# Gate sums inside the score products of the first four heads, and other edits to the opening of a fused attention and two-layer kernel

## The chip, the cores and the metric

The kernel runs on one core of one Trainium2 chip, and the metric is the device time of one launch in microseconds (us). The core has TensorE (PE in the rows; its weight loads are PEld), VectorE (DVE), ScalarE (ACT), GpSimd (POOL) and SyncE (SP), whose queue issues nearly all of the DMAs. Each engine takes its instructions in the order in which the program gives them.

## The reference, cut to what matters

```python
scores = scale * np.matmul(q, k.transpose(0, 1, 3, 2))      # q, k: [4, 8, 576, 64], scale = 1/8
cum = np.cumsum(np.log(np.clip(f, 0.0001, 1.0)), axis=-1)   # f: [4, 8, 576], the gates
decay = cum[:, :, :, None] - cum[:, :, None, :]
scores = np.where(causal, -1e9, scores + decay)
attn = softmax(scores)                                      # the row maximum is subtracted first
x = matmul(attn, v)                                         # heads side by side: [2304, 512]
x = leaky_relu(x @ w_in, 0.01) @ w_out                      # moe_: 512 x 2048, 2048 x 512
return silu(x @ w_in2) @ w_out2                             # moe2_: the same sizes
```

The gate term of a query (`cum` at its own row) is the same for all keys of that row, so it falls out of the softmax; only the term of the key changes the result.

## The kernel before, in words

The program is written out by a planner (`Plan`): generators for each part of the work yield steps with an engine, an estimated cost and a rank, and a simulated clock decides the order in which the steps of one engine are emitted (a lower rank first, then the earlier request). The hardware then runs each engine in that order and waits on semaphores. A changed cost, rank or wait can so change the order of everything behind it.

Attention goes by batch and half of the sequence: the first 256 tokens (blocks of 128 queries with 128 and 256 keys) and the last 320 tokens. The first eight heads (`load_first`, n < 8) are the first half of batch 0. They are loaded in pairs into tiles `qk` with 66 rows: 64 rows of q or k and two rows for the gates. `gates` loads f (`fs`), clamps it on VectorE (line 351), takes logarithms on ScalarE (line 353) and multiplies by a triangle of 8.0 (`tri`, made by GpSimd in lines 333 and 334) on TensorE (line 368). That gives `cps`, 8 times the cumulative sums: two chunks of 128 tokens for the first 256 columns, five chunks for the last 320, as each half sums from token 0. `first_rows` copies the sums of the first half to `cfr` (lines 419 and 420) and sends them by eight small DMAs (line 132) into rows 64 and 65 of the `qk` tiles. A score product (`product` in `score`, line 606) is then one fp32 matmul over 66 rows. VectorE masks it and takes the row minimum (line 594), ScalarE the exponential (line 624), VectorE or ScalarE scales it (lines 632 and 634), TensorE transposes it (line 683), and a pair of heads is multiplied with v (line 752) and split into two parts into `ring` (lines 288 and 296).

`plain_rows` and `split_rows` store the sums of all 32 heads for the later heads (`cum_p`, `cum_d`), with copies on ScalarE and the other steps on GpSimd. When they are through, `gates` gives its tiles back, and room for the second weight matrix opens (`wo`).

`first_weights` brings 32 weight tiles of 512 KB, 16 of w_in and 16 of w_out, once the gate rows are sent (`wait("rows")`). Each is rebuilt to fp32 by `to_f32` (ScalarE line 1351, VectorE lines 1352, 1353 and 1355). The 16 tiles of w_in and the first two of w_out are then split into a rounded part (ScalarE, line 288) and a remainder (`less`: GpSimd line 295 or VectorE line 296, whichever the planner takes to end first). The first layer (`hidden`, line 882, and `summed`, lines 954 and 960) takes steps as weights and tokens come, beside the attention of the next heads. The second layer follows from about 600 us.

Of the kernel before, what the change touches and what calls it, by code (L numbers as in the profile page):

```python
# [34 lines left out]
C_LEAD = 3  # L35
FAVOR = 0.3
# [192 lines left out]
def fused_kernel(ctx, tc, qt, kt, va, vb, ft, w1, wi2, wo2, out):  # L229
# [69 lines left out]

    def build_consts():  # L300
        def mask(t, pattern, cmp, fill, base, mult):
            return lambda: nc.gpsimd.affine_select(
                out=t, in_=t, pattern=[pattern], compare_op=cmp, fill=fill, base=base, channel_multiplier=mult
            )

        for r in range(2):
            yield op("pool", 0.3, lambda: nc.gpsimd.memset(cum_rows[0][r][:, 1 - r], 1.0))
        signal("ones")
        yield op("pool", 0.6, lambda: nc.gpsimd.memset(zmask, 0.0))
        yield op("pool", 0.75, mask(zmask, [-1, ZOFF + 256], ALU.is_ge, -8.0 * MASK, ZOFF, 1))  # L310
        signal("zmask")
        for st in stats:
            yield op("pool", 0.1, lambda: nc.gpsimd.memset(st[:, 6:9], 1.0))
        yield op("pool", 0.15, lambda: nc.gpsimd.memset(ident, 1.0))
        yield op("pool", 0.25, mask(ident, [-1, 128], ALU.is_equal, 0.0, 0, 1))
        signal("ident")


    cum_rows = {}

    def gates(cp):
# [4 lines left out]
        tri = cp.tile([128, 512 + S], F32, name="tri")  # L326
# [4 lines left out]

        def triangle():
            yield op("pool", 0.95, lambda: nc.gpsimd.memset(tri, 8.0), 0)
            yield op("pool", 1.05, lambda: nc.gpsimd.affine_select(
                out=tri, in_=tri, pattern=[[1, 512 + S]], compare_op=ALU.is_ge,
                fill=0.0, base=-512, channel_multiplier=-1,
            ), 0)
# [9 lines left out]
        def logs(n, sl):  # L347
            src = ft[0:nfull * 128, :].rearrange("(c p) h -> p c h", p=128) if n == 128 else ft[nfull * 128:S, :]
            dst = fs[0:n, sl, :] if n == 128 else fs[0:n, nfull, :]
            yield dma(100e3, lambda: nc.sync.dma_start(out=dst, in_=src), 0)  # L350
            yield dve(64, lambda: nc.vector.tensor_scalar(
                fs[0:n, sl, :], fs[0:n, sl, :], 0.0001, 1.0, op0=ALU.max, op1=ALU.min), 0)
            yield act(128, lambda: nc.scalar.activation(fs[0:n, sl, :], fs[0:n, sl, :], ACTF.Ln), 0)

        yield par(warm_up(), triangle(), logs(*parts[0]), logs(*parts[1]))
        p.start(seq(op("act", 1.4, lambda: nc.scalar.activation(warm, fs[0:1, 0, 0:1], ACTF.Exp), 0)))
        pss = []
        banks = []
        for i, (t0, tn) in enumerate(HALF):
            banks.append((yield take(("av", "sp")[i], (1, 3)[i])))  # L360
            ps = ps_at.tile([H * B, tn], F32, tag=("av", "sp")[i], name="cps", bufs=(1, 3)[i])
            todo = [c for c in range(nfull + 1) if 128 * c < t0 + tn]

            def sums():
                for c in todo:
                    n = 128 if c < nfull else rem
                    o = 512 - 128 * c + t0
                    nc.tensor.matmul(  # L368
                        ps, fs[0:n, c, :], tri[0:n, o:o + tn], start=(c == todo[0]), stop=(c == todo[-1])
                    )  # L370

            yield op("pe", 2 * pe_cost(tn, 4) * len(todo), sums, 0)
            pss.append(ps)
            if i == 0:
                cf = cum_rows[0]
                p.start(first_rows(ps, cf))
        signal("cum")

        def plain_rows():
            yield pool(S, lambda: nc.gpsimd.memset(cp3[:, 1, :], 1.0))  # L380
            for i, ((t0, tn), ps) in enumerate(zip(HALF, pss)):
                w = slice(t0, t0 + tn)
                yield act(tn, lambda: nc.scalar.copy(cp3[:, 0, w], ps))
                if i == 0:
                    yield wait(("cf", 0), ("cf", 1))
                give(("av", "sp")[i], banks[i])
                yield pool(tn / 2, lambda: nc.gpsimd.tensor_scalar(
                    cp3[:, 2, w], cp3[:, 0, w], -1.0, 1.0, op0=ALU.mult, op1=ALU.mult))
# [3 lines left out]
        def split_rows():  # L392
            c, hi, lo = cp3[:, 0], cr[:, 0], cr[:, 1]
            yield pool(S, lambda: nc.gpsimd.memset(f32(cr[:, 2:4, :]), 1.0))
# [8 lines left out]
        yield from split_rows()  # L403
        signal("gates")

    def first_rows(ps, cf):

        def rows(r, step):
# [6 lines left out]
            ) for i in range(H // 2)])  # L415
# [3 lines left out]
            rows(0, act(256, lambda: nc.scalar.copy(cf[0][:, 0], ps[0:H]), 0)),  # L419
            rows(1, dve(256, lambda: nc.vector.tensor_scalar(cf[1][:, 1], ps[0:H], -1.0, None, op0=ALU.mult), 0)),  # L420
# [32 lines left out]
    def load_first():  # L453
# [3 lines left out]
        def group(i):  # L457

            t = first[i] = slot(i, [66, 2, 2, tn], F32, "qk0")
            def move(r, src):  # L460
                yield dma(131e3, lambda: nc.sync.dma_start(
# [1188 lines left out]
```

## Time and profile before

| | us |
|---|---|
| median of 3 runs | 1010.4 (1008.49 to 1010.43) |
| the profiled execution's own time | 1006.94 |
| its span, first to last instruction | 1005.2 |
| TensorE busy in it | 989.9 |
| VectorE, ScalarE, GpSimd busy | 772.9, 637.3, 141.1 |

Times in rows are us from the span's start unless marked ns. An fp32 matmul shows as two MATMUL records. "Busy" of TensorE is modelled from instruction ends, and it says nothing of the clock; the granted clock (PEclk) stands beside it, with 1.00 for 2.4 GHz and 0.50 for 1.2 GHz. In a timeline, the name behind "<-" in brackets is what ended the idle time before the piece.

### The profile page before, as it was taken

The numbers are of one execution on the slowest core, as the hardware profiler recorded it, in microseconds if no ns is written. First come the engines' busy times: TensorE is split into PE (matmuls) and PEld (weight loads), VectorE is DVE, ScalarE is ACT, GpSimd is POOL, SyncE is SP. The second block draws the span as 40 slices with busy tenths as digits, with TensorE's granted clock in tenths as the row PEclk, the third lists the DMA queues.
The fourth block names the chain that finished last, engine by engine and source line by source line (L and its number), as shares of the span: only waits on it lengthen the run. The fifth ranks groups of instructions, "written<-read, shape, count | busy, mean of one in ns | idle before, by whom it ended". The sixth has DMA issues, their size and how long they took to land.

```text
span 1005.2 us, 20884 instructions
## 1 busy us (share of the span) xinstructions
PE 989.9 (98%) x7786; PEld 943.5 (94%) x7786; DVE 772.9 (77%) x1818; ACT 637.3 (63%) x1385; POOL 141.1 (14%) x161
## 2 busy tenths in 40 slices
PE   8999999999999999999999999999999999999998
PEld 5667779999999999999999999999999999999997
DVE  4899867787788878878776989685832389998884
ACT  5666667767887678877774657565644576444441
POOL 2232002211222211342110212000000000000000
PEclk8799999999999999999999999999999999999999
DMA  5943423231242222332221876688873486445441
GB/s 166 339 125 108 170 69 109 75 97 41 62 131 77 68 72 58 100 97 70 85 70 69 272 269 235 216 293 315 293 254 134 158 292 181 147 142 153 126 127 63
DMA packets 98213, 148.98 MB, mean 148 GB/s; under 512 B 8296, under 2 KB 69376, under 8 KB 96032
## 3 DMA queue, kind: packets, MB, share of 16 engines
q1 hardware_dynamic: 98112, 147.65, 45.8%
q8 instruction: 61, 1.00, 0.4%
q14 instruction: 40, 0.33, 0.1%
HBM read 99.21 MB, written 43.66 MB: 142 GB/s over the span
## 4 chain that ended last, share of the span: by engine, by line
PE 89%; DVE 6%; issue 2%; ACT 1%; POOL 0%; DMA 0%; DVEq 0%; ACTq 0%; POOLq 0%
PE hps L882 19%; PE m L1317 18%; PE m L1161 18%; PE acc L960 17%; PE sps L606 6%; PE tps L683 5%; PE av L793 4%; PE acc L954 2%; PE av L752 1%; DVE ct L1353 1%; DVE sc L594 1%; DVE ct L1355 1%; PE cps L368 1%; DVE ct L1352 1%; DVE sc L632 1%
## 5 line engine op out<-in xcount | busy, mean ns | idle before, releaser
L882 PE MATMUL hps<-ring,w 128*128 128x256 f32 x1728 | 261.1, 288 | 0.0
L882 PEld LDWEIGHTS hps<-ring,w 128*128 128x128 f32 x1728 | 229.5, 192 | 5.5 <-issue 3.5
L960 PE MATMUL acc<-g,dec 128*128 128x256 f32 x1344 | 199.2, 285 | 1.4 <-DVE dec L296 1.4
L1161 PE MATMUL m<-xc,w 128*128 128x256 f32 x1536 | 185.4, 282 | 1.4 <-ACT u L1193 0.7
L1161 PEld LDWEIGHTS m<-xc,w 128*128 128x128 f32 x1536 | 184.2, 191 | 1.8 <-ACT u L1193 0.9
L1317 PE MATMUL m<-w,gc 128*128 128x256 f32 x1512 | 181.6, 283 | 0.0
L1317 PEld LDWEIGHTS m<-w,gc 128*128 128x128 f32 x1512 | 181.3, 191 | 0.2 <-DVE gc L296 0.2
L960 PEld LDWEIGHTS acc<-g,dec 128*128 128x128 f32 x1344 | 177.4, 191 | 2.0 <-DVE dec L296 1.6
L288 ACT CAST gc<-g 128x512 fp32r<-128x512 f32 (+1 forms) x144 | 80.0, 566 | 82.5 <-DVE g L1008 32.6
L624 ACT ACTIVATE sc<-sc,st 128x576 f32<-128x576 f32 (+4 forms) x160 | 93.1, 582 | 56.3 <-DVE st L594 54.8
L288 ACT CAST dec<-wo 128x512 fp32r<-128x512 f32 x112 | 69.4, 620 | 44.2 <-PE acc L960 42.8
L296 DVE TENSOR_TENSOR gc<-g,gc 128x512 fp32r<-128x512 f32 (+1 forms) x144 | 87.5, 619 | 12.4 <-ACT gc L288 11.1
L594 DVE CUSTOM_DVE_ANT_0 sc<-sps,zmask 128x288 f32<-128x288 f32 (+4 forms) x160 | 71.9, 450 | 30.2 <-PE sps L606 28.6
L683 PE MATMUL tps<-ident,sc 66*107 66x66 f32 (+3 forms) x480 | 70.4, 275 | 4.6 <-DVE st L643 2.1
L296 DVE TENSOR_TENSOR dec<-wo,dec 128x512 fp32r<-128x512 f32 x82 | 57.1, 697 | 20.7 <-ACT dec L288 20.3
L683 PEld LDWEIGHTS tps<-ident,sc 66*107 66x107 f32 (+3 forms) x480 | 56.4, 155 | 11.7 <-issue 3.5
L1008 DVE TENSOR_TENSOR g<-g 128x256 f32<-128x256 f32 x144 | 59.1, 419 | 7.2 <-DMA g<-g_d 6.3
L701 DVE TENSOR_TENSOR pl<-tps,pt 107x320 fp32r<-107x320 f32 (+2 forms) x114 | 54.2, 507 | 12.4 <-ACT pt L700 11.6
L295 POOL TENSOR_TENSOR dec<-wo,dec 128x512 fp32r<-128x512 f32 x30 | 42.7, 1423 | 145.1 <-ACT dec L288 120.0
L606 PE MATMUL sps<-m,s 68*128 68x288 f32 (+9 forms) x264 | 60.0, 308 | 0.1
L700 ACT CAST pt<-tps 107x320 fp32r<-107x320 f32 (+2 forms) x114 | 45.9, 446 | 16.8 <-PE tps L683 16.5
L296 DVE TENSOR_TENSOR g<-hps,g 128x512 fp32r<-128x512 f32 x65 | 44.6, 686 | 13.7 <-ACT g L288 13.1
(132 smaller groups left out, 1397.2 us busy)
## 6 DMA issues: line engine op xcount, KB each, us to landing
g_d<-z SPq DMA_DIRECT2D x16, 1024.0 KB
g<-g_d SPq DMA_DIRECT2D x32, 512.0 KB
w_d<-f SPq DMA_DIRECT2D x16, 896.0 KB
ws<-w_d SPq DMA_DIRECT2D x56, 256.0 KB
wst<-in_wi_dram SPq DMA_DIRECT2D x16, 512.0 KB
wst<-in_wo_dram SPq DMA_DIRECT2D x16, 512.0 KB
qk<-in_kt_dram SPq DMA_DIRECT2D x24, 288.0 KB
wss<-in_w_dram SPq DMA_DIRECT2D x10, 512.0 KB
```

Source lines behind the costliest of these rows:

```text
L288: ("act", act_cost(n, base), lambda: nc.scalar.copy(dst, src), 0.0),
L296: ("dve", dve_cost(n), lambda: nc.vector.tensor_tensor(dst, a, b, op=ALU.subtract), 0.0),
L594: yield dve(w, lambda: nc.vector.tensor_tensor_reduce(out=sc[0:qn, k0:k0 + w], in0=ps[0:qn], in1=zmask[0:qn, z0:z0 + w], scale=-0.125, sca ...
L606: nc.tensor.matmul(ps[0:qn], ht[x][:, qs], ht[y][:, k0:k0 + w], start=r == 0, stop=r == len(ops) - 1)
L624: yield act(kn, lambda: nc.scalar.activation(sc[0:qn, 0:kn], sc[0:qn, 0:kn], ACTF.Exp, scale=-1.0, bias=st[0:qn, 2 * i + a:2 * i + a + 1], ...
L683: nc.tensor.transpose(ps[0:k1 - k0, o:o + qn], ht["p"][i][0:qn, k0:k1], ident[0:qn, 0:qn])
L701: yield op("dve", dve_cost(width), lambda: nc.vector.tensor_tensor(pts[1][0:kw], ps[0:kw], f32(pt[0:kw]), op=ALU.subtract), 0, PE_LAT)
L882: nc.tensor.matmul(hp_t[:, part], w[:, wi, c * 128:(c + 1) * 128], x[xi][:, c, :], start=(part == 0 and c == 0 and r == 0), stop=(c == KC ...
L960: nc.tensor.matmul(o, w[:, wi, c * 128:(c + 1) * 128], g[:, gi, part * T:(part + 1) * T], start=(start and r == 0 and c % 2 == 0), stop=(s ...
L1008: ("dve", dve_cost(n), lambda: nc.vector.tensor_tensor(dst, a, b, op=op_), 0.0),
L1161: nc.tensor.matmul(dst[:, a], w[:, wi, c * 128:(c + 1) * 128], x[:, xi, c], start=start and a == 0 and c == 0 and r == 0, stop=stop and c ...
L1317: nc.tensor.matmul(banks[b][:, e], t[:, gi, a * 128:(a + 1) * 128], w[:, wi], start=begin and a == 0 and r == 0, stop=jp == NP // 2 - 1 an ...
```

## The change

For the first four heads (`DIRECT = 4`) a score product no longer reads gate rows. It takes the 64 rows of q and k, and then adds into the same PSUM bank, for each chunk of 128 keys, a matmul whose stationary operand is the logarithm column of that head spread over all queries, and whose moving operand is the triangle, now -8. The `qk` rows are sent for heads 4 to 7 only. The sums `cps` take only the chunks that begin in their own half; the last value of the first half is added afterwards on VectorE. GpSimd clamps f, and VectorE fills tiles that GpSimd filled before; GpSimd no longer takes remainders of weight tiles (`less(..., "d")`) nor the work on the rows for later heads, which VectorE and ScalarE do. One load of f and one of k are issued by ScalarE. Two tiles of w_in (`EARLY = 2`) are sent once heads 2 and 3 and the first v are sent, the others still after "rows". The end of `gates` also waits for the scores of the fourth head.

```diff
+DIRECT = 4
+EARLY = 2
 def build_consts():
+            yield from clamp(0)      # GpSimd: tensor_scalar max, min on fs
+            yield from clamp(1)
 def gates(cp):
-        tri = cp.tile([128, 512 + S], F32, name="tri")
+        tri = cp.tile([128, HALF[1][1]], F32, name="tri")
-            todo = [c for c in range(nfull + 1) if 128 * c < t0 + tn]
+            todo = [c for c in range(nfull + 1) if t0 <= 128 * c < t0 + tn]
-            yield op("pe", 2 * pe_cost(tn, 4) * len(todo), sums, 0)
+                yield op("pe", pe_cost(tn - lo, 4), sums, 0 if i == 0 else 1)
+                    yield dve(tn, lambda: nc.vector.tensor_scalar(
+                        cp3[:, 2, w], ps, cp3[:, 2, t0 - 1:t0], None, op0=ALU.add), 0)
-            yield pool(S, lambda: nc.gpsimd.tensor_tensor(lo, c, f32(hi), op=ALU.subtract))
+            yield dve(S, lambda: nc.vector.tensor_tensor(lo, c, f32(hi), op=ALU.subtract))
-                yield pool(S / 2, lambda: nc.gpsimd.tensor_scalar(dst, f32(src), -1.0, 1.0, op0=ALU.mult, op1=ALU.mult))
+                yield act(S, lambda: nc.scalar.mul(dst, f32(src), -1.0))
+        yield wait(("scored", DIRECT - 1, 1))
 def first_rows(ps, cf):
-            ) for i in range(H // 2)])
+            ) for i in range(DIRECT // 2, H // 2)])
 def load_first():
+                if i == 0 and r:
+                    yield op("act", 0.6, lambda: nc.scalar.dma_start(out=dst, in_=src_), 0, 2.0)
-            yield wait(("row", 0, i), ("row", 1, i))
+            if 2 * i >= DIRECT:
+                yield wait(("row", 0, i), ("row", 1, i))
 def product(ps, k0, w):
+            if n < DIRECT:
+                nc.tensor.matmul(ps[0:qn], ht["s1"][0:64, qs], ht["m1"][0:64, k0:k0 + w], start=True, stop=False)
+                for c in range(w // 128):
+                    nc.tensor.matmul(
+                        ps[0:qn, 128 * c:w], opened["fs"][:, c, n:n + 1].broadcast_to([128, qn]),
+                        opened["tri"][:, 0:w - 128 * c], start=False, stop=c == w // 128 - 1,
+                    )
+                return
 def conv_in(f):            # and in conv_out for f < RES
-        yield less(DM, w[:, 1], t, f32(w[:, 0]))
+        yield less(DM, w[:, 1], t, f32(w[:, 0]), "d")
 def first_weights():
-        yield wait("rows")
-
         def fetches(which):
+            if which:
+                yield wait("rows")
             for f in range(FF):
+                if f == EARLY:
+                    yield wait("rows")
                 yield from fetch(f, which)
+        yield wait(("prep", DIRECT - 1), "v0_sent")
```

## Rows read from the trace of the kernel before

**Rows 1.** The page, first part: busy us, share of the span, instructions.

```profile
PE 989.9 (98%) x7786; PEld 943.5 (94%) x7786; DVE 772.9 (77%) x1818; ACT 637.3 (63%) x1385; POOL 141.1 (14%) x161
```

**Rows 2.** Stretches: length; PE, PEld, DVE, ACT, POOL busy (count); clock, DMA share, GB/s.

```profile
10.70:16.50 5.80, 4.49 (x23) 2.90 (x22) 3.91 (x21) 4.47 (x17) 1.92 (x3) 0.97 0.36 98
16.50:26.20 9.70, 9.70 (x41) 6.77 (x41) 6.48 (x31) 7.07 (x24) 0.32 (x1) 0.50 0.88 293
26.20:29.90 3.70, 1.80 (x14) 1.08 (x13) 3.34 (x13) 3.32 (x11) 3.30 (x3) 0.96 1.02 363
29.90:43.20 13.30, 13.08 (x38) 7.67 (x39) 9.86 (x30) 7.34 (x19) 1.27 (x1) 0.50 1.01 341
43.20:60.00 16.80, 16.68 (x108) 12.84 (x107) 16.72 (x37) 12.80 (x26) 5.95 (x3) 0.99 0.48 155
60.00:100.00 40.00, 39.09 (x222) 28.14 (x222) 39.13 (x87) 26.05 (x58) 11.12 (x8) 1.00 0.47 137
200.00:300.00 100.00, 100.00 (x833) 99.77 (x832) 81.45 (x234) 76.31 (x197) 21.77 (x33) 1.00 0.30 85
```

**Rows 3.** Timeline of TensorE, 4 to 45 us: start, us, what, count.

```profile
4.63 6.12 PE L368 MATMUL cps<-tri,fs 128*32 128x256 f32 x14 [0.87 <-ACT fs L353]
10.68 2.15 PE L606 MATMUL sps<-qk 66*128 66x128 f32 x8
...
14.50 0.83 PE L606 MATMUL sps<-qk 66*128 66x128 f32 x4
15.17 0.49 PE L683 MATMUL tps<-ident,sc 128*128 128x128 f32 x3
...
24.48 1.49 PE L606 MATMUL sps<-qk 66*128 66x128 f32 x4
25.76 0.78 PE L683 MATMUL tps<-ident,sc 128*128 128x128 f32 x3
...
27.13 0.87 PE L752 MATMUL av<-pf,v 128*64 128x256 f32 x8
30.12 0.87 PE L683 MATMUL tps<-ident,sc 128*128 128x128 f32 x3 [2.12 <-DVE st L643]
...
40.58 2.93 PE L882 MATMUL hps<-ring,w 128*128 128x256 f32 x12
```

**Rows 4.** Timeline of SP and VectorE in the opening: clamps, gate rows, mask, weights.

```profile
2.78 1.38 DVE L351 TENSOR_SCALAR fs<-fs 128x128 f32<-128x128 f32 x2 [1.57 <-DMA fs<-in_ft_dram]
...
7.00 5.10 SPq L132 DMA_DIRECT2D qk<-cfr  x8
...
11.33 0.29 DVE L594 CUSTOM_DVE_ANT_0 sc<-sps,zmask 128x128 f32<-128x128 f32 x1 [3.97 <-PE sps L606]
...
18.58 1.96 SPq L1393 DMA_DIRECT2D wsr<-in_w_dram  x4
```

**Rows 5.** Groups of GpSimd over the span, by form: the splits of weights.

```profile
L295 POOL TENSOR_TENSOR w<-ct,w 128x512 fp32r<-128x512 f32 x11 | 17.9, 1629 | 51.8 <-ACT w L288 51.8
L295 POOL TENSOR_TENSOR wr<-ct,wr 128x512 fp32r<-128x512 f32 x1 | 1.8, 1802 | 2.6 <-ACT wr L288 2.6
```

**Rows 6.** Groups of VectorE, 20 to 130 us, by form: conversion and split.

```profile
L1353 DVE SCALAR_TENSOR_TENSOR ct<-cy,ct 128x512 int32<-128x512 int32 x16 | 12.9, 809 | 0.0
L1353 DVE SCALAR_TENSOR_TENSOR ct<-wo,ct 128x512 int32<-128x512 int32 x14 | 11.7, 837 | 0.2
L1355 DVE SCALAR_TENSOR_TENSOR ct<-wss,ct 128x512 int32<-128x512 int32 x10 | 9.0, 904 | 0.1
L296 DVE TENSOR_TENSOR w<-ct,w 128x512 fp32r<-128x512 f32 x5 | 3.4, 687 | 1.5 <-ACT w L288 1.5
```

**Rows 7.** Timeline: one GpSimd split, and VectorE instructions during and after it.

```profile
61.46 1.39 POOL L295 TENSOR_TENSOR w<-ct,w 128x512 fp32r<-128x512 f32 x1 [1.33 <-ACT w L288]
61.65 1.75 DVE L1353 SCALAR_TENSOR_TENSOR ct<-wo,ct 128x512 int32<-128x512 int32 x1
63.76 0.68 DVE L1353 SCALAR_TENSOR_TENSOR ct<-cy,ct 128x512 int32<-128x512 int32 x1
```

More of the change, by code (lines that the diff above doesn't have):

```diff
@@ L297, in less @@
         ) if c[0][0] in engines], rank, lat)
+    opened = {}
     def build_consts():
[L301 to L316, printed above, removed]
+        tri, fs = opened["tri"], opened["fs"]
+        def zero(cost, t, value, rank=0):
+            return op("dve", cost, lambda: nc.vector.memset(t, value), rank)
@@ new lines, in keep, with masked, clamp @@
+        def keep(cost, t, step, cmp, fill, base, rank=0):
+            return op("pool", cost, lambda: nc.gpsimd.affine_select(
+                out=t, in_=t, pattern=[[step, t.shape[-1]]], compare_op=cmp, fill=fill, base=base,
+                channel_multiplier=-step,
+            ), rank)
+        def masked(c0, c1):
+            return keep((c1 - c0) * 1.1e-3, zmask[:, c0:c1], -1, ALU.is_ge, -8.0 * MASK, ZOFF - c0)
+        def clamp(k):
+            n, sl = opened["parts"][k]
+            yield wait(("fs", k))
+            yield op("pool", 0.35, lambda: nc.gpsimd.tensor_scalar(
+                fs[0:n, sl], fs[0:n, sl], 0.0001, 1.0, op0=ALU.max, op1=ALU.min), 0)
+            signal(("clamped", k))
@@ new lines, in build_consts, with fills @@
+        z0, z1 = ZOFF - 128, ZOFF + 128
+        def fills():
+            yield zero(0.3, tri, -8.0)
+            signal("tri_set")
+            yield zero(0.2, zmask[:, z0:z1], 0.0)
+            signal("zmask0_set")
+            for st in stats:
+                yield zero(0.08, st[:, 6:9], 1.0)
+            signal("stats")
+            yield zero(0.12, ident, 1.0)
+            signal("ident_set")
+            for r in range(2):
+                yield zero(0.25, cum_rows[0][r][:, 1 - r], 1.0)
+            signal("ones")
@@ new lines, in selects @@
+        def selects():
+            yield wait("tri_set")
+            yield keep(0.35, tri, 1, ALU.is_ge, 0.0, 0)
+            signal("tri")
+            yield wait("zmask0_set")
+            yield masked(z0, z1)
+            signal("zmask0")
+            yield from clamp(0)
+            yield from clamp(1)
+            yield wait("ident_set")
+            yield keep(0.25, ident, -1, ALU.is_equal, 0.0, 0)
+            signal("ident")
+            for c0, c1 in ((0, z0), (z1, ZOFF + 256)):
+                yield op("pool", (c1 - c0) * 0.9e-3, lambda: nc.gpsimd.memset(zmask[:, c0:c1], 0.0), 0)
+                yield masked(c0, c1)
+            signal("zmask")
+            for t in opened["ones"]:
+                yield op("pool", 0.6, lambda: nc.gpsimd.memset(t, 1.0), 0)
+            signal("rows_set")
@@ L319, in fused_kernel @@
+        yield par(fills(), selects())
     cum_rows = {}
@@ L330, in gates @@
         z = cp.tile([128, 256], F32R, name="z")
[L332 to L337, printed above, removed]
+        opened.update(tri=tri, fs=fs, parts=parts, ones=(cp3[:, 1, :], f32(cr[:, 2:4, :])))
         def warm_up():
@@ L476, in values, with send @@
             t = first["v"] = slot(H // 2, [128, H, va.shape[3], D], F32, "v0")
-            yield dma(524e3, lambda: nc.sync.dma_start(out=t, in_=va[0].rearrange("h p c d -> p h c d")), 0)
+            def send():
+                nc.sync.dma_start(out=t, in_=va[0].rearrange("h p c d -> p h c d"))
+                signal("v0_sent")
+            yield dma(524e3, send, 0)
             signal("v0")
@@ L590, in least @@
             z0 = ZOFF - q0 + k0
-            yield wait("zmask")
+            yield wait("zmask" if half else "zmask0")
             if a:
@@ L616, in score @@
                 ps = ps_at.tile([128, w], F32, tag="sp", name="sps")
-            yield op("pe", pe_cost(w, 4 if plain(n) else 2), lambda: product(ps, k0, w), 0, 0.05)
+            if n < DIRECT:
+                yield wait("tri", ("logs", 0))
+            cost = pe_cost(w, 4 if plain(n) else 2)
+            if n < DIRECT:
+                cost += sum(pe_cost(w - 128 * c, 4) for c in range(w // 128))
+            yield op("pe", cost, lambda: product(ps, k0, w), 0, 0.05)
             p.start(least(a, ps, k0, w, bank))
@@ L1425, in conv_out @@
             yield copy(DM, w[:, 0], t)
-            yield less(DM, w[:, 1], t, f32(w[:, 0]))
+            yield less(DM, w[:, 1], t, f32(w[:, 0]), "d")
             give("gtmp", i)
@@ L1583, in opening @@
         p.start(gates(cp), after_gates)
-        p.start(build_consts())
         yield from load_first()
```

54 lines of the change are left out of this document (33 added, 21 removed).

## The prediction

> **What bounds the kernel now.** I read the busy shares first. TensorE is busy for 989.9 us of the span [rows 1], so no other engine's total can set the time; the question is where TensorE is slow or waits. The table of stretches answers that [rows 2]: from 200 to 300 us it is busy 100.00 us at full clock with its weight loads at 99.77, with nothing to win. All that is left lies ahead of that. From 16.5 to 26.2 us and from 29.9 to 43.2 us the granted clock is 0.50, the lower of the two levels (1.2 instead of 2.4 GHz): 23.0 us that would be 11.5 at the higher. From 26.2 to 29.9 it works 1.80 of 3.70 us. From 43.2 to 100 us the clock is back, but VectorE is busy 16.72 of 16.80 and 39.13 of 40.00 us: the rebuilding of weights sets the pace, and TensorE's apparent 98% hides short gaps, since ends are modelled.
>
> The timeline says why the opening is late [rows 3, 4]. The sums `cps` hold TensorE from 4.63 to 10.75 us; their first part is copied and sent to the heads by eight DMAs that SP issues from 7.00 for 5.10 us; the first score product starts at 10.68 and the first mask at 11.33 us. Weight tiles wait in the same queue until 18.58 us. The first step of the first layer (`hps`) comes at 40.58 us. After about 100 us TensorE sets the end, so whatever lets VectorE leave its saturated stage earlier moves the end about one for one.
>
> **The change part by part.**
>
> *Sums and rows at the start.* The seven matmuls of `cps` stream 2 x 256 + 5 x 320 = 2112 columns in 6.12 us, 2.9 ns a column, mostly at the low level [rows 3]. Of these 384 + 576 = 960 stay, and the second 576 have a lower rank. The first mask no longer needs `cps`, its copies or the row DMAs, only f, its logarithm, the triangle and the first q and k. The clamps ended at 4.16 us [rows 4] and `cps` began at 4.63. On GpSimd I take the clamps between half their present 1.38 us and the same, so a start of the first product between 4.2 and 5.0 us; I take 4.6 for the 384 columns of `cps` or the product, whichever the plan puts first. With 1.1 us for the 384 columns at 2.9 ns, the first mask stands at about 6.1 instead of 11.33: 5.2 us earlier; bounds 3.9 to 6.
>
> *Three more matmuls per head.* A head's old product has 128 + 256 = 384 columns and takes 0.67 us at full clock (14.50 to 15.17) and 1.28 at half (24.48 to 25.76) [rows 3]: 1.74 and 3.33 ns a column. Added are 128 for the first block and 256 + 128 for the second, 512 a head, 0.89 or 1.71 us; for four heads 3.6 or 6.8 us. The second part of `cps`, 576 columns, adds 1.0 to 1.9 us among them. What covers this is the softmax beside it: over 9.7 us, some 1.76 pairs of 5.5 us, ScalarE works 7.07 and VectorE 6.48 us [rows 2], about 4 us a pair, while a direct pair takes TensorE about 2.5 + 1.8 = 4.3 us at full clock (2.5 is half of the 5 us that a pair takes at the low level). So with a full clock I cost the products at 1.7 us of the 5.2: the last values product of the eight heads, which ends at 28.0 us [rows 3], comes 3.5 us earlier. At half clock the cover is gone; that is a rival below.
>
> The Trainium skill (TensorE: Matmul & The Clock Gate, Part 1: The HAM clock gate) says that the low clock is the default, that sustained matmul activity releases it and an idle engine brings it back. The trace agrees only in part: the clock is low from 29.9 us, after the idle 2.12 us before 30.12, yet it stayed at 0.50 for 9.7 and 13.3 us of recorded full work [rows 2, 3]. So I do not count on denser products to keep the clock up; what that would give is the second rival.
>
> *Loads and early tiles.* SP loses four row DMAs (5.10 / 8 = 0.64 us each) and two loads that ScalarE issues: 3.8 us. Everything behind, the weights from the third tile on included, is sent about 4 us earlier. The two early tiles (1.05 MB) go out at about 5 us instead of 18.58. At 363 GB/s [rows 2] they hold the DMA engines for 2.9 us. Behind them lie the rows and loads of heads 4 to 7; these are wanted by the third pair, not before 5 + 2 x 4.3 = 13.6 us, and should land by 12. Cost nothing; without that cover up to 2.9 us.
>
> What the early tiles bring: rebuilding and splitting one takes VectorE lines 1352, 1353, 1355 and 296. Undisturbed, 1353 and 296 take 0.68 and 0.69 us [rows 6, 7]; with the other two at most at that, an estimate, one tile is 2.1 to 2.7 us, two about 5.0. VectorE is idle for 1.9 + 3.2 + 0.4 + 3.4 = 8.9 us between 10.7 and 43.2 [rows 2]. Two tiles filled in there are worth between 0 (if the plan's order puts other waits in front of them) and 5.0 us. I take 1.5, nearer to nothing, since that idle time is made of short waits for scores in a queue that keeps its order.
>
> *Splits off GpSimd.* Twelve splits (11 and 1) go from GpSimd to VectorE [rows 5]. Each costs VectorE its 0.69 us less the overlap of neighbours, 0.6: 12 x 0.6 = +7.2 us. But while GpSimd runs one, VectorE instructions stall: 1.75 against 0.68 us [rows 7]. Over the stage the groups show (809 - 680) x 16 + (837 - 680) x 14 + (904 - 680) x 10 ns = 6.5 us of excess [rows 6], and at one full stall of 1.07 for each split it would be 12.8. So the move is worth between +0.7 and -5.6 us; I take -2.0.
>
> *Work on rows for later heads.* ScalarE gets two passes and VectorE about two that GpSimd had, at some 0.6 us each. They have a low rank, the ninth head wants them only behind the 28.0 us, and ScalarE has 2.6 + 6.0 us free in the two half-clock stretches [rows 2]: nothing; without that cover 1.2 us on VectorE. The wait for the fourth head's scores holds only the end of `gates` and comes by 13.6 us, ahead of the weight tiles that need that room (18.58 and later before). On GpSimd the identity and the rest of the mask now queue behind the clamps, which wait for f at 2.78; the first transposes want them two products and a softmax later, near 9 us. Both nothing; if the identity were late, its delay past 9 us would be paid once, at most the 1.4 us of the clamps.
>
> **The sum.** -3.5 (opening) - 1.5 (early tiles) - 2.0 (splits) = -7.0 us. From the bounds: at best -6.0 + 1.7 = -4.3, -5.0 and -5.6, about -15; at worst -3.9 + 3.4 = -0.5, 0 and +0.7, about 0 with the clock as before. The profiled execution took 1006.94, so it would take 999.9; the median of the runs shown is 3.5 us above it, so I predict 1003.4 us for the median.
>
> **Rivals.**
>
> *The low clock takes the direct heads (slower).* The place is 5 to 37 us. At 1.2 GHz a direct pair takes 5.5 + 3.4 = 8.9 us: 5.0 + 2 x 8.9 + 2 x 5.5 + 1.9 for `cps` + 1.3 for the tail = 37.0 against 28.0, 9.0 us late. Of that VectorE's work on early tiles (at most 5.0) and the splits (2.0) give back up to 7: between +2 and +9, I put it at +2.6, as VectorE fills the time with weights: 1013.0. For it: 9.7 us at 0.50 in this very stage. Against: the clock was up from 10.7 to 16.5 (0.97) behind a dense stretch. It decides if the clock falls before the second pair; from a last product of the eight heads at about 33 us on, the gain is gone.
>
> *Work fills the second low stretch (much faster).* With two tiles ready early, `hps` can start soon after the eight heads, near 27 instead of 40.58 us, and keep TensorE at work from 26 to 43. If the clock then stays up, the 13.3 us at 0.50 give back up to 6.6: about 7.0 + 6 = 13 us in all, 997.4. Against: `hps` needs more tiles at once, and these come at VectorE's pace.
>
> *The opening is hidden anyway (no change).* From the third tile on, weights still wait for "rows" and for room, and VectorE has no free time from 43.2 to 100 us. If its saturated stage ends where it did because 7.2 us are added there, less 6.5 given back, only some 1 us is left: 1009.4. The edits would then do what they say, on a path that sets nothing.
>
> **How the numbers follow.** Forecast 0.52, much faster 0.16, no change 0.16, slower 0.16. The forecast's own range is 998.5 to 1007. About 0.2%, 2 us, is what can be told from no change. Faster: 0.52 x 0.97 + 0.16 + a little of the third = 0.69; same 0.16; slower 0.15. The range of 995 to 1012 leaves about one in ten on either side.
>
> **What would show it.** Right: the first mask near 6 us; the last values product of the eight heads near 24.5; weight tiles from about 5 us, the others from about 14; no GpSimd work between 15 and 140 us, and line 1353's mean back near 0.68; VectorE out of saturation some 7 us earlier, about 93 instead of 100. Wrong: a clock of 0.50 over the direct heads and a last product after 33 us, or VectorE saturated until the same time as before, or a gap of TensorE after 200 us that was not there, as the plan's order changes behind the opening too.

## The result, and the profile after

The changed kernel took 1012.57 us in the median of 7 runs (1012.12 to 1017.23), the kernel before 1009.46 (1007.57 to 1010.43) in 7 runs beside it. The ratio is 1.0051, with a 95% interval of 1.0036 to 1.0066: about 5 us slower, where 7 us faster was forecast. That is the place of the first rival, the low clock over the direct heads (1013.0). The profiled execution took 1012.12 us, its span 1010.4. Single runs of one kernel lie up to 15 us apart in this study, so profiles are set beside their own execution's time, and verdicts and differences go by the ratios. The two medians lie 3.1 us apart, less than the ratio says.

The page's first part after the change answers to [rows 1]:

```profile
PE 994.6 (98%) x7806; PEld 948.6 (94%) x7806; DVE 773.3 (77%) x1848; ACT 639.2 (63%) x1390; POOL 101.0 (10%) x130
```

The stretches answer to [rows 2] (length; PE, PEld, DVE, ACT, POOL busy; clock, DMA share, GB/s):

```profile
5.27:18.00 12.73, 12.73 (x32) 6.58 (x32) 2.41 (x12) 3.64 (x14) 1.80 (x3) 1.00 0.50 158
18.00:31.90 13.90, 11.09 (x64) 7.31 (x63) 12.81 (x53) 10.98 (x35) 0.00 (x0) 1.00 0.88 265
31.90:52.00 20.10, 19.79 (x69) 13.37 (x69) 12.80 (x39) 14.00 (x34) 0.00 (x0) 0.50 0.91 312
60.00:100.00 40.00, 39.72 (x238) 29.05 (x238) 37.12 (x92) 26.49 (x60) 0.00 (x0) 1.00 0.39 111
200.00:300.00 100.00, 99.92 (x829) 99.19 (x828) 84.08 (x240) 79.29 (x202) 20.51 (x30) 1.00 0.30 85
```

From 200 to 300 us nothing has changed. The loss lies ahead of that: counted back from the end, the same number of matmul records remains between 4 and 6 us later than before at every point from 70 to 400 us (5.9 at 70, 4.1 at 100, 4.9 at 275, 5.5 at 400). It is there at 70 us and is then only carried.

TensorE's timeline of the opening answers to [rows 3] (start, length, what):

```profile
1.26 2.50 PE L383 MATMUL wps<-z 128*128 128x256 f32 x10 [1.26 <-DVE z L379]
5.27 0.79 PE L666 MATMUL sps<-qk 64*128 64x128 f32 x2 [1.51 <-DMA qk<-in_kt_dram]
5.99 0.79 PE L668 MATMUL sps<-tri,fs 128*128 128x128 f32 x2
6.72 1.06 PE L417 MATMUL cps<-tri,fs 128*32 128x256 f32 x2
7.71 1.22 PE L666 MATMUL sps<-qk 64*128 64x256 f32 x2
8.86 1.65 PE L668 MATMUL sps<-tri,fs 128*128 128x256 f32 x4
10.44 0.64 PE L417 MATMUL cps<-tri,fs 128*32 128x128 f32 x2
11.00 0.79 PE L666 MATMUL sps<-qk 64*128 64x128 f32 x2
...
17.16 0.90 PE L757 MATMUL tps<-ident,sc 128*128 128x128 f32 x3
...
18.33 0.48 PE L666 MATMUL sps<-qk 64*128 64x128 f32 x2
18.75 0.49 PE L668 MATMUL sps<-tri,fs 128*128 128x128 f32 x2
19.16 0.70 PE L666 MATMUL sps<-qk 64*128 64x256 f32 x2
19.79 0.92 PE L668 MATMUL sps<-tri,fs 128*128 128x256 f32 x4
...
31.66 1.09 PE L757 MATMUL tps<-ident,sc 128*128 128x128 f32 x3 [1.66 <-ACT sc L708]
...
34.60 1.55 PE L826 MATMUL av<-pf,v 128*64 128x256 f32 x8
...
47.46 2.91 PE L956 MATMUL hps<-ring,w 128*128 128x256 f32 x12
```

Read the steps from one start to the next. A piece of two records of 128 columns takes 0.72 us up to 18 us (5.27 to 5.99) and 0.42 after it (18.33 to 18.75). So the level is the lower one until about 18 us, although the column of the granted clock reads 1.00 there: the trace's record of the clock begins only at 18.27 us, with the upper level, and the column counts the time before as 1.00. A direct head takes 1.45 + 2.73 = 4.18 us at the lower level (5.27 to 6.72, 7.71 to 10.44) and 2.2 at the upper. Before, the level was up by 9 us, in the run of `cps` (the record begins at 9.28); now it is low from the start to 18 and again from 31.9 to about 52. The last values product of the eight heads ends at 36.1 instead of 28.0, and `hps` starts at 47.46 instead of 40.58.

SP's queue and VectorE in the opening, against [rows 4]; first SP:

```profile
4.08 1.05 SPq L1467 DMA_DIRECT2D wsr<-in_w_dram  x2
11.50 2.69 SPq L134 DMA_DIRECT2D qk<-cfr  x4
...
21.94 0.42 SPq L1467 DMA_DIRECT2D wsr<-in_w_dram  x1
```

```profile
6.95 0.29 DVE L655 CUSTOM_DVE_ANT_0 sc<-sps,zmask 128x128 f32<-128x128 f32 x1 [4.41 <-PE sps L668]
...
10.55 0.42 DVE L655 CUSTOM_DVE_ANT_0 sc<-sps,zmask 128x256 f32<-128x256 f32 x1 [3.30 <-PE sps L668]
...
16.49 0.42 DVE L655 CUSTOM_DVE_ANT_0 sc<-sps,zmask 128x256 f32<-128x256 f32 x1 [3.03 <-PE sps L668]
```

The first mask did come early, at 6.95 instead of 11.33. But VectorE then waits for scores again and again: it works 2.41 of the 12.73 us to 18.00. Gate rows and third weight tile are later than before (7.00 and 18.58).

VectorE's groups from 20 to 130 us, against [rows 6]:

```profile
L298 DVE TENSOR_TENSOR w<-ct,w 128x512 fp32r<-128x512 f32 x16 | 10.9, 682 | 0.9 <-ACT w L290 0.9
L1427 DVE SCALAR_TENSOR_TENSOR ct<-cy,ct 128x512 int32<-128x512 int32 x16 | 10.9, 681 | 0.1
L1427 DVE SCALAR_TENSOR_TENSOR ct<-wo,ct 128x512 int32<-128x512 int32 x11 | 7.5, 684 | 0.0
L1429 DVE SCALAR_TENSOR_TENSOR ct<-wss,ct 128x512 int32<-128x512 int32 x10 | 6.9, 685 | 0.1
```

The stalls beside GpSimd's splits are gone: 681 to 685 ns instead of 809 to 904.

### The profile page after: what moved, and what is told of

Same layout as the page of the kernel before. It is cut to its first block, busy times and chain, and to the rows that moved or that the text cites. A ratio compares the mean times of both kernels' runs of the same rounds, so it can differ in the third digit from the quotient of the medians.

```text
span 1010.4 us, 20864 instructions
## 1 busy us (share of the span) xinstructions
PE 994.6 (98%) x7806; PEld 948.6 (94%) x7806; DVE 773.3 (77%) x1848; ACT 639.2 (63%) x1390; POOL 101.0 (10%) x130
## 4 chain that ended last, share of the span: by engine, by line
PE 79%; DVE 3%; ACT 1%; issue 1%; DMA 1%; POOL 0%; SPq 0%; DVEq 0%; ACTq 0%; POOLq 0%
PE m L1391 18%; PE m L1235 17%; PE acc L1034 16%; PE hps L956 16%; PE sps L675 4%; PE av L867 4%; PE tps L757 4%; PE acc L1028 1%; DMA ws<-w_d 1%; DVE w L298 1%; DVE xc L298 0%; PE av L826 0%; DVE g L298 0%; DVE dec L298 0%; DVE f L1082 0%
## 5 line engine op out<-in xcount | busy, mean ns | idle before, releaser
L298 DVE TENSOR_TENSOR dec<-wo,dec 128x512 fp32r<-128x512 f32 x90 | 63.2, 703 | 14.7 <-ACT dec L290 13.8
L297 POOL TENSOR_TENSOR vh<-v,vh 128x320 fp32r<-128x320 f32 (+1 forms) x42 | 31.5, 750 | 307.9 <-DVE vh L291 170.0
```

What stands on the lines that cost most here:

```text
L298: ("dve", dve_cost(n), lambda: nc.vector.tensor_tensor(dst, a, b, op=ALU.subtract), 0.0),
```

## The experiments

My theory after the result: the direct heads cost all of the loss and more, because they run at TensorE's lower level, with three more matmuls each. Rivals: the gate rows of heads 4 to 7 come too late; the moved splits cost VectorE more than thought; the early tiles delay loads. Every run below was timed in five rounds; "ratio" is to the kernel before, timed beside it. A ratio is known to between 0.1 and 0.3%, so a difference of two is known to some 2 or 3 us.

**Splits alone.** The kernel before, with only the splits moved:

```diff
-yield less(DM, w[:, 1], t, f32(w[:, 0]))
+yield less(DM, w[:, 1], t, f32(w[:, 0]), "d")
```

> The kernel before with one edit: the twelve remainders of weight tiles go to VectorE, none to GpSimd. My price: 2 us faster than before (12 x 0.6 us more work on VectorE, but the stalls of 0.6 to 1.1 us beside each GpSimd split are gone), about 1007.5. Rival: VectorE is the bound from 43 to 100 us and gains nothing, or loses: within 1 us of before, or up to 3 us slower.

Measured: 1006.11 us, ratio 0.9980 (0.9965 to 0.9996), a gain of 2.0 us. The splits are not the loss.

**No direct heads.** The changed kernel with `DIRECT = 0`, and the waits on direct heads dropped:

```diff
-DIRECT = 4
+DIRECT = 0
```

> The changed kernel with DIRECT = 0: all eight heads take their gate rows again, all other edits stay. Products theory (TensorE's own time in the opening, 2.2 us more or less per direct head at the high clock and 4.2 at the low one, pushes the eighth head's last values product from 28.0 to 36.1 us and the end by 5 us): that product ends by 28 us, and the time is 3 to 6 us under the kernel before, about 1004 to 1006, since splits and early tiles still help. Rows theory (what is late is the sums, copied at 11.1 instead of 6.5 us, and behind them the loads of heads 4 to 7 and the third weight tile): the same, as the sums are then undisturbed; the run with the sums first tells the two apart. If the loss lies in the other edits (splits, early tiles, work on the rows for later heads), the time stays near 1012.

Measured: 1005.31 us, ratio 0.9959 (0.9938 to 0.9979). The rest of the change gains 4.1 us; the direct heads turn that into a loss of 5.1, so they cost 9.2 (6.1 by the medians). This is the fastest version of the study by its ratio. And it gets there with a later opening (the last values product of the eight heads ends at 33.6 us, where 28 was expected):

```profile
4.11 3.44 PE L417 MATMUL cps<-tri,fs 128*32 128x256 f32 x10 [0.34 <-ACT fs L396]
11.67 3.37 PE L674 MATMUL sps<-qk 66*128 66x128 f32 x8 [4.12 <-DMA qk<-cfr]
...
32.05 1.55 PE L825 MATMUL av<-pf,v 128*64 128x256 f32 x8
44.14 4.52 PE L955 MATMUL hps<-ring,w 128*128 128x256 f32 x18
```

That is TensorE's timeline of it. The first product waits 4.12 us for gate rows that lie behind the two early tiles, and the level is low from about 10 to 48 us. An early first mask is not what the end hangs on. And this version has some 37 us at the lower level.

**Two direct heads.** `DIRECT = 2`:

> The changed kernel with two direct heads (DIRECT = 2) instead of four. With all four the time is 1.0051 of before, with none 0.9959. Products theory, with a price per head: halfway, about 1.000 of before (1008). Rival (the whole loss comes from the first two heads, which run at the low clock): at 1.003 or more. Rival (it comes from the order that follows on four): at 0.997 or less.

Measured: 1014.19 us, ratio 1.0040 (1.0024 to 1.0056), but 1006.29 in the profiled execution. In the median, two direct heads lose nearly what four do, so it is no price per head. Where the median execution loses them is not shown, as the profile is of another.

**Sums ranked first.** The sums for all heads get a rank ahead of the products:

```diff
-yield op("pe", pe_cost(tn - lo, 4), sums, 0 if i == 0 else 1)
+yield op("pe", pe_cost(tn - lo, 4), sums, -1)
```

> The changed kernel with all five sum matmuls ranked ahead of the products on TensorE, so that the rows for heads 4 to 7 leave by about 7 us. Products theory: TensorE has the same work, the eighth head's last values product stays at 34 us or later and the time at 1011 to 1014. Rows theory: the third weight tile goes out at 18 us or earlier instead of 21.9, and the time falls to the kernel before or under it, 1005 to 1009.

Measured: 1019.51 us, ratio 1.0085 (1.0055 to 1.0116), slower than both expectations. The order that was meant did not come about: in the profile one of the five sums (`cps`, 3.93 us) runs ahead of the first product, the others still between products, the last at 16.12. The rows are sent at 7.78 instead of 11.50 and the third weight tile at 19.93 instead of 21.94, yet the kernel is slower, with the spacing of the lower level up to about 57 us in the profile. So earlier rows alone do not win the loss back; what they would be worth at the same level this run does not say.

**More warm-ups.** `WARM = 20` instead of 10, and then 24 at a rank ahead of everything. In both, the planner put only 14 ahead of the first product and spread the others between the products.

> The changed kernel with 20 warm-up matmuls instead of 10, so that TensorE isn't idle between 3.8 and 5.3 us. Clock theory (the idle 1.51 us ahead of the first product leaves TensorE at the low level until 18 us, and that is what the opening loses): a direct head takes 2.2 instead of 4.2 us from 9 us on, the eighth head's last values product ends by 30 us, and the time is 1008 or less. Products theory without the clock: the level still changes near 18 us, and the time stays at 1011 to 1014.

> The changed kernel with 24 warm-up matmuls, all ahead of the first product, so that TensorE works without a gap from 1.3 us and the first product starts near 6.5 instead of 5.3. Clock theory: full-height matmuls in a row raise the level near 9 us, as the sums did in the kernel before; then heads 0 and 1 cost 2.2 instead of 4.2 us each, and the eighth head's last values product ends near 32 instead of 36.1: 1008 to 1010. Products theory without the clock: the level still changes near 18 us and the time rises by the added 1 us or so, 1013 to 1014.

Measured: 1018.8 us, ratio 1.0111 (1.0087 to 1.0136), and 1010.78, ratio 1.0019 (0.9990 to 1.0048; single runs from 1003.2 to 1018.4). With 20 the idle time before the first product shrinks from 1.51 to 0.60 us, and the steps still change only at 19 us; with 24, at 23.7. So a shorter gap did not bring the level up. The first is slower than both of its expectations, the second lies between its two. They did not test a dense block, since there was none.

**Direct heads without their sums.** Heads 0 to 3 leave out the gate-sum matmuls, so their gates are missing from the output; the order of everything else stays.

```diff
-for c in range(w // 128):
+for c in ():
```

> The changed kernel in its own order, but the direct heads leave out the gate sums: the score product of heads 0 to 3 is the one matmul over 64 rows, and their gates are missing from the result. Products theory: the three matmuls themselves take 2.3 us a head at the low clock (0.73 + 1.58) and 1.2 to 1.3 at the high one, 7 us for the four; without them the eighth head's last values product ends by 30 us, hps starts by 42, and the time is 5 to 8 us under the changed kernel, 1003 to 1007. Order or clock theory (the three matmuls only fill time that is lost anyway, to the low clock or to late loads): 1010 or more.

Measured: 1009.27 us, ratio 1.0000 (0.9987 to 1.0013), between the two expectations: 5.1 of the 9.2 us go with the added matmuls. VectorE, ScalarE and GpSimd have the same instructions in the same order as in the changed kernel. TensorE's timeline:

```profile
5.21 0.80 PE L666 MATMUL sps<-qk 64*128 64x128 f32 x2 [1.46 <-DMA qk<-in_kt_dram]
5.94 1.06 PE L417 MATMUL cps<-tri,fs 128*32 128x256 f32 x2
...
31.89 1.55 PE L826 MATMUL av<-pf,v 128*64 128x256 f32 x8
...
44.74 2.81 PE L956 MATMUL hps<-ring,w 128*128 128x256 f32 x12
```

The steps are those of the lower level until 44 to 47 us, longer than in the changed kernel, and still the last values product ends 2.7 us earlier (33.4 instead of 36.1; by 30 was expected). VectorE works 6.32 us from 5.27 to 18.00 where it worked 2.41. So the gain is that of the matmuls and not of the level. What is left, 4.1 us against gate rows, the direct heads cost without them.

**One block of warm-ups.** The changed kernel, with the warm-ups as one step that nothing can come between:

```diff
-WARM = 10
+WARM = 30
-for _ in range(WARM):
-    yield op("pe", 0.21, lambda: nc.tensor.matmul(wps, z[:, 0:128], z, ...), 0, 0)
+yield op("pe", 0.21 * WARM, lambda: [nc.tensor.matmul(wps, z[:, 0:128], z, ...) for _ in range(WARM)], -2, 0)
```

> The changed kernel with 30 warm-up matmuls of TensorE as one unbroken block ahead of everything, instead of 10: 7.5 us from 1.25 on, by the 0.25 us of one in the trace, so the first product starts near 8.8 instead of 5.27. Theory A (most of the loss is the added matmuls and the order; the lower level in the direct heads only a part): the level is up when the first product starts, a direct head costs 2.3 us at once instead of 4.2, last values product of the eight heads 2 to 4 us earlier than 36.1, end 1008 to 1011. Theory B (the lower level at the first two direct heads is the whole remainder of 4 us): last values product near 32, 1006 to 1008. Rival C (these warm-ups do not raise the level at all): level low as before to 18 us and longer, everything 3.5 us later: 1014 to 1017.

Measured: 1007.66 us, ratio 0.9997 (0.9980 to 1.0014), 5.4 us better than the changed kernel. Its TensorE timeline:

```profile
1.26 5.93 PE L383 MATMUL wps<-z 128*128 128x256 f32 x30 [1.26 <-DVE z L379]
7.12 0.49 PE L666 MATMUL sps<-qk 64*128 64x128 f32 x2
7.53 0.49 PE L668 MATMUL sps<-tri,fs 128*128 128x128 f32 x2
7.95 0.62 PE L417 MATMUL cps<-tri,fs 128*32 128x256 f32 x2
8.50 0.70 PE L666 MATMUL sps<-qk 64*128 64x256 f32 x2
9.12 0.92 PE L668 MATMUL sps<-tri,fs 128*128 128x256 f32 x4
...
29.91 1.55 PE L826 MATMUL av<-pf,v 128*64 128x256 f32 x8
...
40.74 1.65 PE L956 MATMUL hps<-ring,w 128*128 128x256 f32 x6
```

The first product starts 1.85 us later than in the changed kernel, at the upper level from its first step (0.41 us), and a direct head takes 2.3 us. The weight load of a piece starts with the piece, as TensorE's loads (PEld) show for the one at 7.53:

```profile
7.53 0.30 PEld L668 LDWEIGHTS sps<-tri,fs 128*128 128x128 f32 x2
```

The last values product of the eight heads ends at 31.4 instead of 36.1, and `hps` starts 6.7 us earlier. The product is where theory B put it (near 32). The time is at the border of the two theories (1006 to 1008 and 1008 to 1011), and its interval reaches into both. So the lower level in the first direct heads can be most of the loss, but this run doesn't show how much of it. The Trainium skill (TensorE: Matmul & The Clock Gate, Part 1: The HAM clock gate) says that activity kept up releases the low clock. This block bears that out; the changed kernel does not by its records, since TensorE shows 12.73 of 12.73 us busy at the lower level.

What the block does for VectorE is in its stretch of the same length (columns as above):

```profile
5.27:18.00 12.73, 12.65 (x62) 8.04 (x61) 7.51 (x27) 7.66 (x25) 1.80 (x3) 1.00 0.54 170
```

VectorE works 7.51 us where it worked 2.41. But the level is not all that differs. The planner counts the block as 30 x 0.21 = 6.3 us where it counted 2.1, and so puts the other engines' steps in another order. Part of the 7.51 is the rebuilding of the early tiles, whose first step is ScalarE's. In the changed kernel that step stands behind the fourth exponential, so ScalarE takes it late, with the tile long there, as that exponential had waited 3.17 us for its scores:

```profile
16.96 0.51 ACT L698 ACTIVATE sc<-sc,st 128x256 f32<-128x256 f32 x1 [3.17 <-DVE st L655]
17.38 0.18 ACT L698 ACTIVATION_READ_ACCUMULATOR sc<-sc,st 128x1 f32 x1
17.47 0.34 ACT L434 COPY cp<-cps 32x256 f32<-32x256 f32 x1
17.72 0.65 ACT L1425 ACTIVATE cy<-wsr 128x512 f32<-128x512 f32 x1
```

With the block the plan puts it behind the first exponential, and it starts as soon as the tile has landed:

```profile
8.51 0.40 ACT L698 ACTIVATE sc<-sc,st 128x128 f32<-128x128 f32 x1 [2.81 <-DVE st L655]
8.82 0.19 ACT L698 ACTIVATION_READ_ACCUMULATOR sc<-sc,st 128x1 f32 x1
9.89 0.67 ACT L1425 ACTIVATE cy<-wsr 128x512 f32<-128x512 f32 x1 [0.88 <-DMA wsr<-in_w_dram]
```

What of the 5.4 us is the level and what is this order, no run here separates.

**Block, and no sums.** To see if the 5.1 and the 5.4 us are one loss or two; as above, the gates of heads 0 to 3 are missing:

> Heads 0 to 3 leave out the matmuls of the gate sums (so their gates are missing), as before, now behind the unbroken block of 30 warm-ups. Without the sums alone the ratio to before fell from 1.0051 to 1.0000, with the block alone to 0.9997. If the two are one loss counted twice (the added matmuls cost what they cost because they run at the lower level), both together give little more than one: 0.998 to 1.000, 1006 to 1009. If they are two losses beside each other, the sum: 0.994 to 0.996, 1002 to 1005.

Measured: 1011.65 us, ratio 1.0021 (1.0009 to 1.0034). The two don't add; together they gain less than either, 3.0 us, and the time is above both expectations. In its profile (1006.72 us in that execution), TensorE without the sums waits 2.24 and 1.45 us for softmax steps between 11 and 16 us, and the granted clock is 0.50 from about 15 to 36 us; with the sums it is 0.50 from 29.9 to 46.9. So it is not a clean sum of two parts. Behind the block, leaving the matmuls out gains nothing (0.9997 with them, 1.0021 without); since the level falls earlier without them, this does not price them at the upper level.

**Block, and two direct heads.**

> Two direct heads instead of four, behind the block of 30 warm-ups. Without the block the ratio was 1.0040, so nearly all the loss lay in the first two direct heads. If the level was what they lost by, two at the upper level cost 2 x 1.6 = 3.2 us above two heads on gate rows, less what the earlier start is worth: 0.996 to 0.998, 1004 to 1006. If late sums are the rest (the gate rows of heads 2 and 3 wait for sums that still come between products): no better than four direct heads behind the block, 0.9995 to 1.002, 1007.5 to 1010.

Measured: 1009.23 us, ratio 1.0001 (0.9992 to 1.0011), inside the second expectation: no better than four. Whether that is due to late sums, as it supposed, this run does not show. Going from four to two gains nothing, with the block or without.

**The early tiles, with direct heads and without.** `EARLY = 0`, first in the changed kernel, then with `DIRECT = 0`:

> The changed kernel with EARLY = 0: no weight tile is sent before the gate rows; everything else of the change stays. With DIRECT = 0 the two early tiles were worth 2.2 us (0.9959 against 0.9981). Theory (they are worth the same beside direct heads, as VectorE finds the same idle time): 1014 to 1016 us, ratio 1.006 to 1.009. Rival (behind direct heads VectorE is not what is late, so the tiles bring nothing, or delay the loads of heads 4 to 7, which landed 2.1 us later than before): 1010 to 1013, ratio 1.003 to 1.005.

> No direct heads and no early tiles: what is left of the change is the sums of new tokens, the work moved between GpSimd, VectorE and ScalarE, and the splits. In the run without direct heads the gate rows were sent from 6.07 us but the first product waited for them until 11.67, behind two weight tiles of 512 KB. Rows-behind-tiles theory: the first product starts near 9 us, and the time is 1 to 3 us under that run, 1002 to 1004. Early-tiles theory (the tiles rebuilt in VectorE's free time are worth more than the late rows): 1 to 3 us over that run, 1006 to 1008.

Measured: 1019.64 us, ratio 1.0110 (1.0085 to 1.0136) beside direct heads; 1006.79, ratio 0.9981 (0.9966 to 0.9995) without them. So leaving the tiles out costs 5.9 us beside direct heads and about 2.2 without, where the intervals overlap. The first expected the same 2.2 or nothing, so both of its expectations missed; the second came out as its early-tiles theory said. In the profile beside direct heads the first tile is rebuilt at 36.13 us, the steps are those of the lower level until 29 us instead of 18, and the granted clock is 0.50 twice later, from 43 to 53 and from 60 to 70 us. So the 5.9 us are not the tiles' worth to VectorE alone.

**Tiles behind the rows.** With `DIRECT = 0` the early tiles go out once the sums are copied, behind the row DMAs; then the same with the block of warm-ups:

```diff
+if f == 0:
+    yield wait(("cf", 0), ("cf", 1))
-    ... bitcast(I32)), 2)
+    ... bitcast(I32)), -1 if f < EARLY and not which else 2)
```

> Like DIRECT = 0 (all eight heads take the gate rows), but the two early weight tiles are sent behind the gate rows, not ahead of them. With DIRECT = 0 the first product waited 4.12 us for rows that lay behind the tiles and started at 11.67; without early tiles it started at 9.10. Theory (early tiles are worth about 2 us to VectorE, and late rows cost something): first product near 9.1 to 9.8, the tiles landed by about 16, median some 1003 to 1005 us, at or below DIRECT = 0 (1005.3; ratio to before 0.993 to 0.996). Rival (VectorE rebuilds the two tiles ahead of the softmax only if they are there by 10 us; the late rows cost nothing): as without early tiles, 0.998, 1006 to 1007.

> All eight heads take the gate rows, tiles behind the rows, and the same block of 30 warm-ups, which ends near 8.8 us. TensorE has to give the gate sums after it, about 3 us at the upper level or 6 at the lower, so the first product comes at 13 to 16 us. If such a block raises the level and that is what the opening lacks: 1000 to 1004 us. If the time that the block takes is simply lost: 1007 to 1011.

Measured: 1010.33 us, ratio 1.0015 (1.0000 to 1.0031), and 1009.83, ratio 1.0010 (0.9996 to 1.0024). Without the block the first product starts at 9.08 as expected, and the end is 5 us later than with the tiles first, later than both expectations. A first product 2.6 us earlier is worth less than tiles at the start. The plan now puts the first rebuild behind eight exponentials (ScalarE, 19.43 us), where with the tiles first it stands ahead of all (10.11); the profile also has a low stretch from 57 to 64 us. Which of the two makes the 5 us is not settled. With the block the first product starts at 11.93, earlier than expected, and the time is that of the second expectation, the block's time simply lost.

**All profiles together.** VectorE's busy time in the first 60 us, from the same view for the changed kernel and each variant of it, beside the span of the same execution:

| kernel | VectorE busy to 60 us | span, us |
|---|---|---|
| DIRECT 0, EARLY 0 | 43.49 | 1002.8 |
| DIRECT 0 | 43.14 | 1004.8 |
| no sums, block | 42.53 | 1005.0 |
| DIRECT 2 | 41.80 | 1004.5 |
| block | 41.64 | 1005.7 |
| DIRECT 2, block | 41.45 | 1005.8 |
| DIRECT 0, tiles behind rows | 40.92 | 1009.7 |
| no sums | 40.64 | 1007.3 |
| the same with block | 40.02 | 1005.7 |
| 20 warm-ups | 38.29 | 1015.9 |
| 24 warm-ups | 37.25 | 1009.8 |
| changed kernel | 36.87 | 1010.4 |
| EARLY 0 | 33.33 | 1017.9 |
| sums ranked first | 28.31 | 1020.6 |

("The same with block" is DIRECT 0 with tiles behind rows.) A straight line through these has a slope of -1.2 us of span for each us of VectorE work done by 60 us (correlation -0.92; with the kernel that has the splits alone, 40.48 and 1004.8, it is -0.91). The window of the changed kernel, and then of the one with the sums ranked first:

```profile
0.00:60.00 60.00, 53.76 (x219) 35.87 (x220) 36.87 (x134) 36.73 (x96) 4.97 (x15) 0.83 0.67 215
```

```profile
0.00:60.00 60.00, 54.91 (x176) 32.83 (x177) 28.31 (x110) 30.87 (x82) 4.96 (x15) 1.00 0.63 203
```

TensorE is busier in the slowest of them: in this stretch its busy time says nothing. DIRECT 0 has the longest low stretch of all that beat the kernel before, and is among the fastest; VectorE has weights to rebuild meanwhile. This is a correlation over profiles and shows no cause: what VectorE has done by 60 us also measures how far the whole kernel has come, and ScalarE's busy time in the same window follows the span nearly as well (-0.89).

The profiles say one thing more of the level. In the nine kernels where TensorE's first work is an unbroken run (10 warm-ups and then at least 10 records of `cps`, or the block of 30), the trace's record of the clock begins with the upper level between 5.0 and 9.3 us. In the seven where products and single sums alternate behind 10 or 14 warm-ups, it begins between 17.9 and 58.1 us. What in the alternation keeps the level down, no run shows.

## Why the prediction was wrong

The failing step is "Three more matmuls per head", with the choice that went into the sum: "with a full clock I cost the products at 1.7 us of the 5.2". Left out, with the other engines' order unchanged, the added matmuls give back 5.1 us. Three things in the step were off.

- *The level.* The prediction took over the clock of 0.97 that [rows 2] show from 10.7 us on. It had even put this clock down to "a dense stretch" ahead of it, and that was the 14 records of `cps` [rows 3], which the change takes apart: four at first, then pieces between products. The level came up at 18 us instead of 9; with a dense block put back it was up at the first product, and 5.4 us came back, part of them perhaps by the changed order.
- *The size.* Columns are not the whole price. The head's 1.28 us at the lower level became 4.18 and its 0.67 at the upper 2.3: +2.9 and +1.6 instead of +1.71 and +0.89. Pieces of 128 columns step by 0.42 us where 128 columns at the row's 1.74 ns make 0.22. A direct head has four pieces with 896 columns, 1.56 us at that price; so each piece costs about 0.2 us more than its columns. Its weight load starts only with it (0.30 us for two, 7.53 in the block's timeline). The 5 us of a pair at the lower level, halved for the cover, is 5.5 in the same sentence of the prediction.
- *The cover.* The softmax beside the products was to hide them. But a slow product starves the softmax, and the weights stand in ScalarE's and VectorE's queues behind it, in fixed order. VectorE, which the prediction itself named as the pace of the next stage, worked 2.41 of 12.73 us, and 6.32 with the added matmuls left out.

A second step failed with it: the sum let the 5.2 us of the early mask, less the products, pass on to the end. Without the added matmuls the direct heads still cost 4.1 us against gate rows, with the first mask early and the last values product at 33.4 us, at the lower level all the way. What these 4.1 us are made of stays open.

The other steps:

- *The first mask near 6 us*: right in kind (6.95; k landed late by 1.51 us of idle time). That the last values product would follow it 3.5 us earlier was wrong: 36.1 us, 8 later. Its own sign of failure, a last product after 33 us, is what came.
- *Splits, -2.0 us*: right, by the run that does this alone (0.4 to 3.5). The stalls went, as it said; that the size fits so well is luck, since it was picked from +0.7 to -5.6.
- *Early tiles, -1.5 us*: 2.2 without direct heads, which can't be told from 1.5; 5.9 beside them, beyond the range of 0 to 5, but with the lower level lasting 11 us longer in that run's profile. Sent at 4.08 as forecast; the first could be used at 9.89 at the earliest.
- *Weights from the third tile about 4 us earlier*: wrong, 21.94 instead of 18.58. They hang on the rows, and the rows on the sums, which now stood between slow products (`cfr` sent at 11.50 instead of 7.00).
- *GpSimd idle between 15 and 140 us, line 1353's mean back near 0.68*: right (rows of the result).
- *VectorE out of saturation near 93 instead of 100*: wrong. From 95 to 110 us it is busy 14.32 of 15 us, before 14.19.
- *The low-clock rival*: right in sign and in what it blames, with a chance of 0.16 that was too small. That its numbers fit is in part luck. It reckoned all eight heads at the lower level (last product at 37.0, measured 36.1), but from 18 to 31.9 us the level was up; and its +2.6, from a range of +2 to +9, counted on VectorE filling the time with weights, which it did not. By the ratio the loss is 5.1. "Against: the clock was up from 10.7 to 16.5" was the row that misled.

The account in sum: splits -2.0 and early tiles about -2.2, together about the -4.1 of DIRECT 0; direct heads +9.2, by runs. Of the 9.2, the block takes away 5.4 and leaving out the matmuls 5.1, and these overlap. What is left, 3.8 us with the block, was not taken apart; the block itself starts the first product 1.85 us later. By the medians the same differences are smaller: 6.1 for the direct heads, 3.8 for the block, 2.4 for the matmuls. Their signs agree, but the sizes are known no better than that.

## What to carry to other kernels

When a change thins out a dense run of matmuls, ask what that run did for TensorE's level, and price what comes behind at the lower one. Price small fp32 matmuls from the steps between records of the same shape, not by columns alone. Where a planner orders the steps by estimated costs, compare the engines' order of two variants before calling their difference the effect of one thing: a block of warm-ups moved weight steps ahead of exponentials. Where a later engine is the pace of the next stage, ask of an edit to the opening how much of that engine's work it lets in, not how early the first product is: here 4.4 us earlier at the first mask came with 5 us later at the end.

## What was not expected of the hardware

- TensorE's level is not told by its busy time: 12.73 of 12.73 us busy at the lower level up to 18 us, and 54.91 of 60 us with the lower level up to about 57 with the sums ranked first, while the level was up at the end of 5.93 us of unbroken warm-ups, where with 14 warm-ups, and products and single warm-ups behind them, it was not before 19 or 23.7 us.
- The granted clock of a profile reads 1.00 until the trace's record of it begins, with steps of 0.72 us where the upper level gives 0.42. The steps between records of one shape tell the level there.
